# Sketched attention and a squared-ReLU layer on one core: full PE tiles, three batches repeated by DMA, a written order

## Chip, cores and metric

The kernel runs on one core of a Trainium2 chip. The metric is device microseconds of one execution. TensorE (PE) multiplies, with weight loads shown apart as PEld; VectorE is DVE, ScalarE is ACT, GpSimd is POOL, and SyncE (SP) issues most DMAs.

## What is computed

There are 4 batches of 4 heads, 1088 tokens, 32 dimensions, R = 8 sketch rows. Attention's output (4352 tokens of 128 values) goes through a layer of 2048 hidden units.

```
phi(x)  = (S1 x) outer (S2 x)                # 64 features per token
kv, z   = sum_t phi(k_t) v_t , sum_t phi(k_t)
x       = (phi(q) kv) / (phi(q) z + 1e-6)    # per head; heads side by side
out     = (relu(x w_in))^2 w_out             # 128 -> 2048 -> 128
```

Attention runs in f32, the layer in bf16.

## The kernel before

`attention(b, ...)` adds the operations of one batch to a graph and `ffn(n, ...)` those of one token block: `SIZES` has 320, seven of 512, and 448. Each operation has a name, the engines that may do it, a cost and a due value. `Graph.run` simulates the engines with these costs and gives the order, once, when the kernel is built; each engine then executes its list in that order.

For one batch the names are these. The loads `ldk`, `ldq`, `ldv` bring K, Q, V. `tk` and `tq` transpose 32 x 32 blocks on DVE. `ksk` (L448) sketches 32 tokens of keys per matmul; `ka` copies one sketch on ACT and `kp` (L466) makes the 64 products. `vp` (L420) packs V beside a column of ones on POOL. `kv` (L485) sums products with V, in pieces of 32 features; `kve` copies the result to `kvz`, and for two batches a second time with its halves swapped to `kvs`.

The queries' features take one of two ways (`MODE`). Batches 0 and 1 ("pe"): `qr` (L528) makes both sketches already repeated to 64 features, with the stationary `SR`; `qa` copies one of them on ACT, `qp` (L546) multiplies on DVE. Batches 2 and 3 ("dma"): `qr` (L559) makes the plain sketches, `ab` (L568) copies them to SBUF, `wr` (L573) stores them to DRAM (`scr`), `rdA` (L582) and `rdB` (L589) read them back repeated into `qp` and `Bq`, and `qp` (L602) multiplies these.

`num` (L626) multiplies 32 tokens by `kvz`; `mx` divides (L651 to L655), `tx` (L667) transposes and `xe` (L672) copies to `xT`. In a block, `m1` (L693) makes 128 hidden units per matmul, `r` (L702) is the relu of two such, `g` (L712) their square, `m2` (L718) adds to one accumulator `o0`; `oe` (L725) transposes it and `st` (L735) stores it. An f32 matmul appears in the trace as two loads and two matmuls.

SP issues its DMAs one after the other, and each waits until the one eight places before it on the hardware queues has ended. Weights come through POOL's queue, after `gate`, which waits for K of batch 0.

Of the kernel before, what the change touches and what calls it, by code (L numbers as in the profile page):

```python
# [15 lines left out]
SEM = 0.035  # L16
SWITCH = 0.095
LOOK = 0.12
LANES = 8
DMA_FIRST = 1.3  # L20
DMA_LAST = 0.75


KSPLIT = False
N_HEAT = 7
W_PARTS = ((0, 1), (1, 2), (2, 4))
K_LOADS = ((0, 16), (16, 34))
Q_LOADS = ((0, 10), (10, 34))
MODE = ("pe", "pe", "dma", "dma")
QGROUPS = (((0, 10), (10, 22), (22, 34)), ((0, 12), (12, 24), (24, 34)), ((0, 24), (24, 34)), ((0, 24), (24, 34)))  # L30
LD_PRI = ({"k": -200, "q": -198.5, "v": -199}, {"k": -30, "q": -29, "v": -28}, {"k": -20, "q": -25, "v": -19}, {"k": -10, "q": -15, "v": -9})
RD_PARTS = ((0, 768), (768, 1088))
LATE = 10
RELU_PEN = 0.6
SQ_PEN = 0.3
SIZES = [320] + [512] * 7 + [448]
STAGE = {"tk": 1, "ksk": 2, "ka": 3, "kp": 4, "kv": 5, "vp": 5, "kve": 7, "tq": 2.5, "qr": 4, "qa": 4.5, "qp": 6, "num": 8,
         "mx": 9, "tx": 9.5, "xe": 10, "wr": 4.6, "rd": 4.7}
FIRST = {"tk": -50, "ksk": -49, "ka": -48, "kp": -46, "kv": -44, "vp": -44, "kve": -43, "tq": -47.5, "qr": -45, "qa": -44.5,
         "qp": -43.5, "num": -42, "mx": -41, "tx": -40, "xe": -39}  # L40
LEAD = 14.0
MARG = 3.0


def VT(b, key):
    if b == 0:
        return FIRST[key]
    s1 = 17.0 * b - MARG
    lead = LEAD + (6.0 if MODE[b] == "dma" and key in ("tq", "qr", "qa", "wr", "rd") else 0.0)
    return s1 - lead + lead * STAGE[key] / 12.0  # L50

CRIT = {"tk0.0", "tk0.1", "ksk0.0", "ksk0.1", "ka0.0", "ka0.1", "kp0.0", "kp0.1", "kv0.0", "kv0.1", "kve0.0", "kve0.1", "kve0.2", "kve0.3",
        "tq0.0", "qr0.0", "qa0.0.0", "qa0.0.1", "qp0.0.0", "qp0.0.1", "num0.0", "mx0.0", "tx0.0", "xe0.0", "m1.0.0"}
CRIT_LOOK = 1.0


class Buf:
    def __init__(self, *kinds):
        self.kinds = kinds
        self.slot = None  # L60
        self.banks = ()
        self.pending = 0


class Op:
    def __init__(self, name, alts, fn, deps, pri, alloc, uses, shape, dma, after):
        self.name, self.alts, self.fn, self.pri = name, alts, fn, pri
        self.deps = [d for d in deps if d is not None]
        self.after = [d for d in after if d is not None]
        self.alloc, self.uses = list(alloc), list(alloc) + list(uses)  # L70
        self.shape, self.dma = shape, dma
        self.look = LOOK
        self.start = self.end = self.eng = None


class Graph:

    def __init__(self, slots):
        self.ops = []
        self.free = {}
        self.kinds = {}
        for kind, names in slots.items():
            self.kinds[kind] = [(n, parts) for n, parts in names]
            for _, parts in names:
                for x in parts:  # L90
                    self.free[x] = [0.0, None]

    def add(self, name, alts, fn, deps=(), pri=0.0, alloc=(), uses=(), shape=None, dma=None, after=()):
        op = Op(name, alts, fn, deps, pri, alloc, uses, shape, dma, after)
        for b in op.uses:
            b.pending += 1
        self.ops.append(op)
        return op

    def slot_time(self, buf, taken=()):  # L100
        best = None
        for kind in buf.kinds:
            for name, parts in self.kinds[kind]:
                if any(x in taken for x in parts) or any(self.free[x][1] is not None and self.free[x][1].pending for x in parts):
                    continue
                t = max(self.free[x][0] for x in parts)
                if best is None or t < best[0] - 0.3:
                    best = (t, name, parts)
        return best

    def run(self):
        eng_free, pipe, shape = {}, 0.0, None
        lanes = []
        todo = {id(o): len(o.deps) + len(o.after) for o in self.ops}
        succ = {}
        for o in self.ops:
            for d in o.deps + o.after:
                succ.setdefault(id(d), []).append(o)
        ready = [o for o in self.ops if todo[id(o)] == 0]
        order = []  # L120
        while ready:
            cands = []
            for o in ready:
                t_slot = 0.0
                ok = True
                taken = []
                for b in o.alloc:
                    s = self.slot_time(b, taken)
                    if s is None:
                        ok = False  # L130
                        break
                    taken += s[2]
                    t_slot = max(t_slot, s[0] + SEM)
                if not ok:
                    continue
                best = None
                for e, (busy, lat, *pen) in o.alts.items():
                    pen = pen[0] if pen else 0.0
                    t = max(eng_free.get(e, 0.0), t_slot)
                    for d in o.deps:  # L140
                        t = max(t, d.end + (SEM if d.eng != e else 0.0))
                    for d in o.after:
                        t = max(t, d.start)
                    if o.dma is not None and e != "POOL" and len(lanes) >= LANES:
                        t = max(t, lanes[-LANES])
                    if e == "PE" and o.shape != shape:
                        t += SWITCH
                    if best is None or t + lat + pen < best[0]:
                        best = (t + lat + pen, t, e, busy, lat)
                cands.append((best[1], o, best))  # L150
            assert cands, "no operation can start: " + ", ".join(o.name for o in ready[:20])
            t0 = min(c[0] for c in cands)
            _, o, (_, t, e, busy, lat) = min(
                (c for c in cands if c[0] <= t0 + c[1].look), key=lambda c: (c[1].pri, c[0]))
            for b in o.alloc:
                _, b.slot, b.banks = self.slot_time(b)
                for x in b.banks:
                    self.free[x] = [t, b]
            o.start, o.end, o.eng = t, t + lat, e
            if o.dma is not None:  # L160
                pipe = max(pipe, t + busy - 0.4 + DMA_FIRST) + o.dma
                o.end = pipe + DMA_LAST
                if e != "POOL":
                    lanes.append(o.end)
            if e == "PE":
                shape = o.shape
            eng_free[e] = t + busy
            for b in o.uses:
                b.pending -= 1
                for x in b.banks:  # L170
                    self.free[x][0] = max(self.free[x][0], o.end)
            ready.remove(o)
            order.append(o)
            for s in succ.get(id(o), ()):
                todo[id(s)] -= 1
                if todo[id(s)] == 0:
                    ready.append(s)
        assert len(order) == len(self.ops)
        self.order = sorted(order, key=lambda o: o.start)
        return self.order  # L180


def act(n):
    return (0.833e-3 * n + 0.053, 0.833e-3 * n + 0.18)


def dve(n, rate=1.042e-3, fix=0.07):
    return (rate * n + fix, rate * n + fix + 0.09)


def pool(n, rate=2.1e-3):
    return (rate * n + 0.12, rate * n + 0.16)


def pe(t):
    return (t, t + 0.17)
# [3 lines left out]
def kernel(  # L200
# [30 lines left out]
    NB = 2  # L231
    NR = 4
# [9 lines left out]
    for i in range(3):  # L242
        for j in range(2):
            tiles[f"h{i}.{j}"] = tiles[f"h{i}"][:, 512 * j : 512 * j + 512]
    for n in ("a0", "o0"):
        tiles[n] = ps.tile([128, 512], F32, name=n, tag=n)
# [543 lines left out]
```

## Time and profile before

| | |
|---|---|
| median of 3 runs | 131.54 us (129.92 to 133.82) |
| profiled execution, span | 132.4 us |
| PE, PEld busy | 103.6, 59.0 us |
| DVE, ACT, POOL busy | 93.4, 81.9, 12.8 us |
| bytes moved by DMA | 15.29 MB, mean 115 GB/s |

The profiled execution is known by its span, from the first to the last instruction; no other time of it was taken. It lies 0.9 us over the median of the runs. The groups of instructions name a line, an engine and an operation, then the number of instructions, busy us and the mean ns of one, and the idle time before them with what ended it. In the chain of waits a row is start, duration and what ran; "issue" is time for which the profile shows no cause. In the table by stretches each engine has its busy us and, in brackets, its instructions; the last three columns are the granted PE clock, the DMA share and GB/s.

### The profile page before, as it was taken

To read this page: it belongs to the slowest core of one execution; us is meant where nothing else is said; L and a number is where in the kernel's file an instruction comes from. 1 tells how busy PE (TensorE), PEld (TensorE's weight loads), DVE (VectorE), ACT (ScalarE), POOL (GpSimd) and SP (SyncE) were. 2 spreads that over 40 slices of the span, in tenths; PEclk is the share of its full clock that TensorE was granted. 3 is DMA by queue.
4 is the path that set the end of the run, shared out by engine and by line. 5 is a ranking of instruction groups with operands and counts; after the bars stand their busy time and mean duration, and the time that the engine had idled before them with its cause. 6 is when DMAs were issued, how large, how long until landed. Compare 5 with 4: busy or idle time off the path is not lost.

```text
span 132.4 us, 4611 instructions
## 1 busy us (share of the span) xinstructions
PE 103.6 (78%) x1979; PEld 59.0 (45%) x1995; DVE 93.4 (71%) x155; ACT 81.9 (62%) x117; POOL 12.8 (10%) x38
## 2 busy tenths in 40 slices
PE   6375297691578898999998699999939789999940
PEld 2074164460544455554553454455434444445410
DVE  2546079795029999889953994997299567899950
ACT  0412017940139896989869419989850299999910
POOL 5492005050310000000000000000000000000000
PEclk9999558999689999999999999999995999999996
DMA  4989999994000030149856306595650220040314
GB/s 120 270 196 341 246 288 301 230 274 94 6 0 5 0 57 7 47 135 242 155 132 160 55 5 124 133 241 153 159 118 5 44 40 0 0 68 11 54 30 69
DMA packets 26596, 15.29 MB, mean 115 GB/s; under 512 B 19792, under 2 KB 24272, under 8 KB 26576
## 3 DMA queue, kind: packets, MB, share of 16 engines
q1 hardware_dynamic: 25152, 13.67, 42.5%
q0 software_dynamic: 992, 1.05, 5.1%
q8 instruction: 15, 0.25, 0.8%
q10 hardware_dynamic: 432, 0.28, 0.7%
q14 instruction: 5, 0.04, 0.1%
HBM read 13.25 MB, written 2.79 MB: 121 GB/s over the span
## 4 chain that ended last, share of the span: by engine, by line
PE 39%; DVE 22%; issue 12%; ACT 10%; DMA 9%; SPq 4%; ACTq 2%; DVEq 0%
PE o L718 10%; DVE g L712 9%; PE h L693 9%; ACT r L702 8%; DVE kp L466 6%; DMA Bq<-scr 5%; PE h L626 4%; PE a L626 3%; PE h L667 3%; SPq L589 3%; DMA S_sb<-in_S_dram 3%; PE a L448 2%; PE h L485 2%; DVE osb L725 2%; PE a L485 2%
## 5 line engine op out<-in xcount | busy, mean ns | idle before, releaser
L702 ACT ACTIVATE r<-h 128x1024 bf16<-128x1024 f32 (+2 forms) x68 | 61.3, 1000 | 5.7 <-PE h L693 5.1
L712 DVE TENSOR_TENSOR g<-r 128x1024 bf16<-128x1024 bf16 (+2 forms) x64 | 40.5, 668 | 6.1 <-ACT r L702 5.3
L718 PE MATMUL o<-g,w_out 128*128 128x512 bf16 (+2 forms) x135 | 38.8, 375 | 3.3 <-DVE g L712 2.0
L693 PE MATMUL h<-xT,w_in 128*128 128x512 bf16 (+2 forms) x137 | 37.9, 369 | 3.9 <-ACT xT L672 1.4
L693 PEld LDWEIGHTS <-w_in 128*128 128x128 bf16 x144 | 15.7, 114 | 18.1 <-issue 6.9
L718 PEld LDWEIGHTS <-w_out 128*128 128x128 bf16 x144 | 13.2, 99 | 18.3 <-issue 8.0
L672 ACT COPY xT<-h 128x768 bf16<-128x768 bf16 (+2 forms) x4 | 2.5, 626 | 14.6 <-PE h L667 14.6
L485 PE MATMUL a<-vp,kp 128*32 128x33 f32 x432 | 5.8, 207 | 4.4 <-issue 4.4
L602 DVE TENSOR_TENSOR qp<-qp,Bq 128x1536 f32<-128x1536 f32 (+1 forms) x4 | 5.2, 1288 | 5.3 <-DMA Bq<-scr 5.3
L485 PEld LDWEIGHTS a<-vp,kp 128*32 128x32 f32 x432 | 5.0, 118 | 6.6 <-issue 6.2
L626 PE MATMUL h<-kvz,qp 128*32 128x66 f32 x260 | 6.1, 242 | 2.2 <-ACT r L702 2.1
L541 ACT COPY A<-h 128x384 f32<-128x384 f32 (+1 forms) x12 | 4.9, 465 | 3.8 <-PE h L528 3.7
L725 DVE STREAM_TRANSPOSE osb<-o 128x512 f32<-128x512 f32 (+2 forms) x9 | 6.1, 682 | 1.5 <-PE o L718 1.5
L710 ACT ACTIVATE g<-r 128x640 bf16<-128x640 bf16 (+1 forms) x8 | 7.1, 900 | 0.1
L420 POOL COPY vp<-vin 128x512 f32<-128x512 f32 x8 | 5.0, 648 | 20.8 <-DMA vin<-in_v_dram 18.7
L626 PEld LDWEIGHTS h<-kvz,qp 128*32 128x32 f32 x260 | 5.2, 122 | 3.8 <-ACT r L702 3.0
L466 DVE TENSOR_TENSOR kp<-h,ka 128x1280 f32<-128x1280 f32 (+1 forms) x4 | 5.7, 1422 | 1.2 <-PE h L485 1.0
L433 DVE STREAM_TRANSPOSE kT<-kin 128x1088 f32<-128x1088 f32 (+2 forms) x5 | 5.3, 1069 | 1.5 <-DMA kin<-in_k_dram 1.5
L466 DVE TENSOR_TENSOR kp<-a,ka 128x1024 f32<-128x1024 f32 (+1 forms) x4 | 5.1, 1285 | 1.5 <-ACT ka L458 1.5
L528 PE MATMUL h<-qT,SR 32*64 32x192 f32 (+1 forms) x192 | 5.9, 358 | 0.2 <-DVE r L704 0.2
L546 DVE TENSOR_TENSOR qp<-h,A 128x384 f32<-128x384 f32 (+1 forms) x12 | 5.9, 518 | 0.0
L485 PE MATMUL h<-vp,kp 128*32 128x33 f32 x144 | 2.4, 230 | 4.4 <-issue 2.7
(61 smaller groups left out, 88.5 us busy)
## 6 DMA issues: line engine op xcount, KB each, us to landing
vin<-in_v_dram SPq DMA_DIRECT2D x14, 128.0 KB
kin<-in_k_dram SPq DMA_DIRECT2D x3, 544.0 KB
qin<-in_q_dram SPq DMA_DIRECT2D x3, 544.0 KB
qp<-scr SPq DMA_DIRECT2D x4, 384.0 KB
Bq<-scr SPq DMA_DIRECT2D x8, 192.0 KB
out_dram<-osb SPq DMA_DIRECT2D x16, 64.0 KB
qp<-scr SPq DMA_DIRECT2D x4, 160.0 KB
Bq<-scr SPq DMA_DIRECT2D x8, 80.0 KB
```

What stands on the lines that cost most here:

```text
L433: nc.vector.transpose(kT[i][:, 32 * c0 : 32 * c1], kin[i][:, 32 * c0 : 32 * c1])
L466: nc.vector.tensor_tensor(out=kp[i][:, j0:j1].rearrange("p j h (x y) -> p (j h) x y", y=R), in0=bb[:, :, None, :].to_broadcast([128, m, R, ...
L485: nc.tensor.matmul(t[p : p + 32, 33 * (h // 2) : 33 * (h // 2) + 33], kp[i][:, j, h, 32 * f : 32 * f + 32], vp[i][:, h, j, :], start=(j == ...
L528: nc.tensor.matmul(at(hb[h // 2])[lo : lo + 64, 512 * half + 256 * x : 512 * half + 256 * x + n], SR[32 * h : 32 * h + 32, x].rearrange("p ...
L546: nc.vector.tensor_tensor(out=qp[i][:, pr, t0 : t0 + 2 * n].rearrange("p (m s) -> p m s", m=2), in0=at(hb[pr]).rearrange("p (m s) -> p m s ...
L626: nc.tensor.matmul(t[32 * cc : 32 * cc + 32, 2 * pr : 2 * pr + 2, :], qp[i][:, pr, 32 * c : 32 * c + 32], (kvs if sw else kvz)[i][:, pr], ...
L693: nc.tensor.matmul(at(hb)[:, step * w : step * w + N], w_in[:, 512 * (ct // E) : 512 * (ct // E) + 512].rearrange("p (c e) -> p e c", e=E) ...
L702: nc.scalar.activation(o, view(at(hb)), ACTF.Relu)
L710: nc.scalar.activation(at(gb)[:, 0 : W * N], r, ACTF.Square)
L712: nc.vector.tensor_tensor(out=at(gb)[:, 0 : W * N], in0=r, in1=r, op=ALU.mult)
L718: nc.tensor.matmul(at(ob)[:, 0:N], w_out[:, ct, :], at(gb)[:, N * w : N * w + N], start=(ct == 0), stop=(ct == CT - 1))
L725: nc.vector.transpose(at(sbuf)[:, 0:N], at(ob)[:, 0:N])
```

## The change

1. **Full tiles.** `ksk` takes 128 tokens per matmul (four of 32 before), `num` 128 tokens (four of 32), `kv` a head's 64 features (two pieces of 32). For this `tk` writes K so that 128 tokens lie side by side, and `kvs` is gone. `qr` of batch 0 takes two heads per matmul with a masked `SR`.
2. **Queries.** Batch 0 alone keeps the PE way, in tiles of 256 tokens. Batches 1 to 3 take the DMA way: one matmul makes both sketches, and the repeats go in two halves (`HALVES`, 18 and 16 chunks of 32 tokens). `rdA` reads the SBUF tile `ab` directly; only the second sketch goes through DRAM.
3. **First loads.** `S0` and the first four quarters of V come from ACT's queue, `S1` from POOL's, K and Q from SP's.
4. **Blocks.** 256, 512, 320, five of 512, 448, 256. Two relus share one square (2048 columns) in the blocks of `Q` = 2; blocks of 256 take four hidden tiles per relu (`W` = 4). All eight PSUM banks are four tiles `h0` to `h3`, and their halves `b0` to `b7`; `m2` accumulates in `b6` and `b7` by turns.
5. **Order.** `Graph.run` is gone. A table `PLAN` names each operation, its engine and its buffer.

```diff
-SIZES = [320] + [512] * 7 + [448]
+BLOCKS = ((256, 4, 1), (512, 2, 2), (320, 2, 2)) + ((512, 2, 2),) * 5 + ((448, 2, 2), (256, 4, 1))
+GROUPS = (((0, 8), (8, 16), (16, 24), (24, 34)),) + (((0, 18), (18, 34)),) * 3
+QTILES = ((0, 8), (8, 16), (16, 24), (24, 32), (32, 34))
+HALVES = ((0, 18), (18, 34))
+PLAN = """
+zero:DVE ldk0.0:SP S1:POOL z0:POOL mk:DVE tk0.0:DVE iota:POOL ident:DVE
...
+        for line in PLAN.split():
+            name, eng, *slots = line.split(":")
...
+            o.fn(eng)
...
             def f_ksk(e, j0=j0, j1=j1, kab=kab):
...
-                    for g in range(4):
-                        c = tok(j, g)
-                        nc.tensor.matmul(
-                            o[32 * g : 32 * g + 32, :, j - j0, :], kT[i][:, 32 * c : 32 * c + 32],
-                            SK.rearrange("p x h r -> p x (h r)"), start=True, stop=True)
+                    lo = 128 * j if j < 8 else 960
+                    nc.tensor.matmul(o[:, :, j - j0, :], kT[i][:, lo : lo + 128],
+                                     SK.rearrange("p x h r -> p x (h r)"), start=True, stop=True)
...
-                        for f in range(2):
-                            p = 64 * (h % 2) + 32 * f
-                            nc.tensor.matmul(
-                                t[p : p + 32, 33 * (h // 2) : 33 * (h // 2) + 33],
-                                kp[i][:, j, h, 32 * f : 32 * f + 32], vp[i][:, h, j, :],
+                        nc.tensor.matmul(
+                            t[64 * (h % 2) : 64 * (h % 2) + 64, 33 * (h // 2) : 33 * (h // 2) + 33],
+                            kp[i][:, j, h, :], vp[i][:, h, j, :],
...
+                            nc.tensor.matmul(
+                                at(hb)[64 * u : 64 * u + 64, 512 * w : 512 * w + n], SK.rearrange("p x h r -> p (x h r)"),
+                                qT[i][:, s0 : s0 + n], start=True, stop=True)
...
+                        dma[e].dma_start(out=qp[i][:, pr, s0 : s0 + n],
+                                         in_=row(u, 0, 2 * pr)[0:16, None, 0:n].to_broadcast([16, R, n]))
...
+                    dma[e].dma_start(out=scr[i][u, :, 0:n], in_=row(u, 1, 0)[0:32, 0:n])
...
-                        for cc in range(4):
-                            c = c0 + 4 * x + cc
-                            if c >= c1:
-                                c -= 2
-                            sw = swap and 2 * (c - c0) >= c1 - c0
-                            nc.tensor.matmul(
-                                t[32 * cc : 32 * cc + 32, 2 * pr : 2 * pr + 2, :],
-                                qp[i][:, pr, 32 * c : 32 * c + 32], (kvs if sw else kvz)[i][:, pr],
-                                start=True, stop=True)
+                        nc.tensor.matmul(t[0:n, 2 * pr : 2 * pr + 2, :], qp[i][:, pr, lo : lo + n], kvz[i][:, pr],
+                                         start=True, stop=True)
```

PE at the front, before: after the warm-up matmuls come batch 0's key sketches (`SK,kT_107`), kv in two runs (`vp_115,kp_119`) around query sketches, and num (`kvz_121,qp_125`).

```order
L448 MATMUL a_66<-SK,kT_107 32x2x32 x16
L448 MATMUL h_65<-SK,kT_107 32x2x32 x20
L485 MATMUL h_65<-vp_115,kp_119 32x33 x32
...
L485 MATMUL h_65<-vp_115,kp_119 32x33 x40
L626 MATMUL a_66<-kvz_121,qp_125 32x66 x9
L626 MATMUL a_66<-kvs_123,qp_125 32x66 x3
```

The same place in the change; `h_63` to `h_66` are the tiles `h0` to `h3`, and the line numbers are those of the new file.

```order
L360 MATMUL h_63<-SK,kT_102 128x2x32 x9
L416 MATMUL h_64<-qT_104,SR 128x256 x4
L386 MATMUL h_63<-vp_108,kp_112 64x33 x16
L266 LDWEIGHTS zero
L266 MATMUL h_66<-zero 128x512
...
L386 MATMUL h_63<-vp_108,kp_112 64x33 x20
L360 MATMUL h_63<-SK,kT_103 128x2x32 x5
L501 MATMUL h_63<-kvz_114,qp_116 128x66 x4
```

Nine key sketches stand for 36, 36 matmuls of kv for 72, and five key sketches of batch 1 now stand between kv and num of batch 0.

SP's queue around the first batch that is repeated by DMA, before (batch 2: `ab_129`, `scr_131`):

```order
L573 DMA scr_131<-ab_129 32x2x272 x4
L582 DMA qp_125<-scr_131 128x1x768 x2
L582 DMA qp_125<-scr_131 128x1x320 x2
L735 DMA out_dram<-osb_81 32x16x32 x4
L589 DMA Bq_127<-scr_131 64x1x768 x4
L589 DMA Bq_127<-scr_131 64x1x320 x4
L735 DMA out_dram<-osb_86 32x8x32 x8
```

And in the change (batch 1: `ab_121`, `scr_123`):

```order
L463 DMA scr_123<-ab_121 32x576
L323 DMA vin_107<-in_v_dram 32x4x256
L303 DMA qin_100<-in_q_dram 128x1088
L323 DMA vin_107<-in_v_dram 32x4x256
L331 DMA vp_109<-in_v_dram 32x4x32 x2
L459 DMA qp_117<-ab_121 128x1x576 x2
L469 DMA Bq_119<-scr_123 64x1x576 x4
L463 DMA scr_123<-ab_121 32x512
L303 DMA kin_99<-in_k_dram 128x1088
L596 DMA out_dram<-osb_69 32x8x32
L323 DMA vin_106<-in_v_dram 32x4x256 x4
L469 DMA Bq_119<-scr_123 64x1x512 x4
```

No store stands between the repeats of one half; loads of V, Q and K of other batches do.

More of the change, by code (lines that the diff above doesn't have):

```diff
@@ L42 @@
[L42 to L53, printed above, removed]
@@ L57 @@
+st6.2624.2:SP m2.9.1:PE g.9.2:ACT:g0 st6.2624.3:SP m2.9.2:PE g.9.3:DVE:g2 m2.9.3:PE st7.3136.0:SP
+oe9:DVE:osb2 st7.3136.1:SP st7.3136.2:SP st7.3136.3:SP st7.3264.0:SP st7.3264.1:SP st7.3264.2:SP st7.3264.3:SP
+st8.3648.0:SP st8.3648.1:SP st8.3648.2:SP st8.3648.3:SP st9.4096.0:SP st9.4096.1:SP st9.4096.2:SP st9.4096.3:SP
+warm:ACT
+"""
 class Buf:
@@ L100, in slot_time @@
[L100 to L180, printed above, removed]
@@ L183, in act, with __init__, add @@
[L183 to L196, printed above, removed]
+    def __init__(self):
+        self.ops = {}
+    def add(self, name, engines, fn, deps=(), alloc=(), uses=(), after=(), **info):
+        assert name not in self.ops, name
+        self.ops[name] = Op(name, engines, fn, deps, after, alloc, uses, info)
+        return self.ops[name]
@@ L256, in at @@
         return tiles[buf.slot]
+    dma = {"SP": nc.sync, "ACT": nc.scalar, "POOL": nc.gpsimd}
+    NB = 2
     eps = 1e-6
@@ L417, in attention @@
+        def f(e):
+            for c in range(2):
+                dma[e].dma_start(out=vp[i][64 + 32 * c : 96 + 32 * c, :, NJ - 1, 0:D], in_=vsrc[:, :, 32 + c, :])
+        o_vt = add(f"ldv{b}.t", "SP", f, [z_ops[i]] + prev(b, "kv"), kind="dma", kb=32, key="vt")
         for a in range(2):
@@ L713, in ffn @@
-            o3 = add(f"g.{n}.{m}", {"DVE": dve(W * N, 0.521e-3, 0.05), "ACT": act(W * N + 40) + (SQ_PEN,)}, f_g, [o2], p - 0.6, alloc=[gb], uses=[rb])
-            def f_m2(e, m=m, gb=gb):
-                for w in range(W):
-                    ct = W * m + w
-                    nc.tensor.matmul(at(ob)[:, 0:N], w_out[:, ct, :], at(gb)[:, N * w : N * w + N],
-                                     start=(ct == 0), stop=(ct == CT - 1))
-            last = add(f"m2.{n}.{m}", {"PE": pe(W * (N / 2400 + 0.0027))}, f_m2, [o3, wo, last], p - 0.7,
-                       alloc=[] if m else [ob], uses=[gb, ob] if m else [gb])
+                    nc.vector.tensor_tensor(out=at(gb)[:, 0 : Q * W * N], in0=r, in1=r, op=ALU.mult)
@@ new lines, in ffn, with f_m2 @@
+            o3 = add(f"g.{n}.{m}", "DVE ACT", f_g, relus, alloc=[gb], uses=[rb], n=Q * W * N, kind="sq")
+            for mm in range(m - Q + 1, m + 1):
+                def f_m2(e, mm=mm, gb=gb):
+                    for w in range(W):
+                        ct = W * mm + w
+                        lo = N * (W * (mm % Q) + w)
+                        nc.tensor.matmul(at(ob)[:, 0:N], w_out[:, ct, :], at(gb)[:, lo : lo + N],
+                                         start=(ct == 0), stop=(ct == CT - 1))
+                wo = o_wout[wpart(W * mm + W - 1)]
+                last = add(f"m2.{n}.{mm}", "PE", f_m2, [o3, wo, last], alloc=[] if mm else [ob], uses=[ob, gb] if mm else [gb],
+                           kind="mm", mm=[(128, N, 1)] * W)
```

616 lines of the change are left out of this document (281 added, 335 removed).

## Prediction

> **What bounds the kernel now.** I read the engine totals first, then stretches of the span, the chain that ended last, and then the gaps on each engine.
>
> ```profile
> PE 103.6 (78%) x1979; PEld 59.0 (45%) x1995; DVE 93.4 (71%) x155; ACT 81.9 (62%) x117; POOL 12.8 (10%) x38
> q8 instruction: 15, 0.25, 0.8%
> ...
> 0.00:21.60 21.60, 12.64 (x350) 8.30 (x351) 10.65 (x23) 4.49 (x12) 9.10 (x30) 0.84 0.94 253
> 21.60:42.00 20.40, 13.27 (x450) 9.42 (x442) 12.24 (x19) 10.31 (x24) 3.72 (x9) 0.92 0.50 117
> 42.00:72.00 30.00, 28.48 (x493) 15.22 (x499) 25.29 (x45) 26.31 (x35) 0.00 (x0) 1.00 0.44 99
> 72.00:106.00 34.00, 28.46 (x604) 16.15 (x611) 26.72 (x42) 20.45 (x27) 0.00 (x0) 0.95 0.47 105
> 106.00:126.30 20.30, 19.73 (x93) 9.67 (x93) 17.21 (x27) 20.30 (x23) 0.00 (x0) 1.00 0.19 31
> 126.30:132.40 6.10, 1.04 (x5) 0.26 (x3) 1.27 (x2) 0.00 (x0) 0.00 (x0) 0.79 0.26 44
> ```
>
> The columns after the stretch are PE, PEld, DVE, ACT and POOL busy. No one engine bounds the whole. Until 42 us, a third of the span, no engine is busy for two thirds of the time; from 42 to 72 PE, DVE and ACT are all nearly full; from 72 to 106 DVE and ACT fall back; then ACT is full until the last relu at 126.3, and 6.1 us are tail. What can be won is therefore idle time at the front and between 72 and 106. Work saved on one engine alone is worth little where three are nearly full.
>
> Of the front, the chain that ended last says this:
>
> ```profile
> 12.23 0.60 PE h L485 x41
> 12.84 2.73 issue
> 15.57 0.71 PE h L485 x33
> ...
> 16.88 1.62 PE a L626 x48
> ...
> 21.01 0.43 PE h L693 x2
> ...
> 30.25 4.38 issue
> 34.63 1.27 PE a L485 x70
> ...
> 35.95 1.32 PE h L626 x47
> ```
>
> Twice PE stops in the middle of one run of equal small matmuls (kv, L485) with nothing to wait for that the profile shows, for 2.73 and 4.38 us. PE has 1979 + 1995 = 3974 instructions and q8 brought 0.25 MB in 15 packets, so a packet is about 260 of them. The DMA view of two stretches, 13.0 to 13.2 and 31.8 to 32.0 us, shows one packet of q8 in each, 2.4 and 2.6 us before PE goes on:
>
> ```profile
> q8 instruction: 1, 0.02, 29.3%
> q8 instruction: 1, 0.02, 41.7%
> ```
>
> I read both stops as PE waiting for its instructions, which it had used up in tiny matmuls.
>
> [...]
>
> **The change, part by part.**
>
> *Front: -3.0.* In the new order PE has 284 f32 matmuls instead of 832. At four records each (two loads, two matmuls), and two for each bf16 one, that is 1874 records for 3990: half the blocks. Up to the first m1 I count about 300, where the old kernel stopped after some 440. The stop at 12.84 should go; at 15.57 PE went on for 0.71, so kv of batch 0 ends 13.6 at the latest and, with fewer, wider matmuls, I say 12.9, not 16.28. From there to the first m1 at 21.01 now pass 4.7 us: kv's copy, num, division, query sketches, transposes, xT's copy. The new order has the same with five key sketches of batch 1 more (5 x 0.17 as priced below, 0.17 that a group adds, and a warm-up matmul: 1.2) and less at half clock (num at 16.88 took 1.62, the same 48 records 0.90 in the rows below): 4.7 + 1.2 - 0.8 = 5.1, so the first m1 at 18.0 us, 3.0 earlier. Bounds: 0, if the loads of V come late instead, and -5. S1 on the POOL queue and V's quarters on ACT I cost at nothing: no row shows a small load on POOL, and ten warm-up matmuls stand ahead of the first key sketch in any case.
>
> *Second stop: -5.5.* The 4.38 us go, and with them the half clock behind them: kv and num at 34.63 and 35.95 took 2.59 us, where the rows below give 0.90 + 0.90 at full clock. That is 6.1 in all; I leave 0.6 for batch 1's V, which loads late in both. Bounds: -6.1, and 0 if V takes the stop's place.
>
> *Repeats by DMA: -4.0.* Batches 2 and 3 now wait for their repeated queries:
>
> ```profile
> 54.41 1.74 SPq L573 DMA_DIRECT2D scr<-ab  x4
> 59.67 2.32 SPq L735 DMA_DIRECT2D out_dram<-osb  x4
> 62.03 5.79 SPq L589 DMA_DIRECT2D Bq<-scr  x8
> 71.60 1.76 DVE L602 TENSOR_TENSOR qp<-qp,Bq 128x1536 f32<-128x1536 f32 x1 [2.63 <-DMA Bq<-scr]
> 74.01 0.59 PE L718 MATMUL o<-g,w_out 128*128 128x512 bf16 x2 [1.81 <-DVE g L712]
> 78.85 0.80 ACT L672 COPY xT<-h 128x768 bf16<-128x768 bf16 x1 [4.54 <-PE h L667]
> 98.12 2.04 PE L626 MATMUL h<-kvz,qp 128*32 128x66 f32 x96 [2.12 <-ACT r L702]
> 104.48 0.80 ACT L672 COPY xT<-h 128x768 bf16<-128x768 bf16 x1 [6.83 <-PE h L667]
> ```
>
> From the first store of the copy ab at 54.41 to the product at 71.60 a batch needs 17.2 us, with four stores ahead of the Bq repeats. PE loses 1.81 + 2.12 = 3.9 us, ACT 4.54 + 6.83 = 11.4. In the change the first 18 of 34 chunks are repeated and used apart, half A comes from the tile ab itself, and ab2 and ab3 stand far ahead of their use. The bounds are 0 and 11.4; I take PE's 3.9, because PE will be the fullest. For batch 1 the same path is new: behind ab1, ACT has ten relus of 1024 columns, seven of 640, two squares and some copies before block 3's first relu, about 18 us at 0.93 and 0.65 us a relu, against 17.2 for a whole batch and less for its first half. It just fits, at no cost.
>
> ```profile
> 57.46 8.39 ACT L702 ACTIVATE r<-h 128x1024 bf16<-128x1024 f32 x9 [0.38 <-PE h L693]
> 41.25 1.29 ACT L702 ACTIVATE r<-h 128x640 bf16<-128x640 f32 x2
> ```
>
> *Squares in pairs: -1.0.* A square of 1024 columns takes 683 ns and one of 896 takes 617, so 1024 more columns are 0.53 us. A pair is 1.21 instead of 1.37, and 27 pairs on DVE save 4.2. DVE is on the path only in part; I take 1.0 (bounds 0 and 4.2).
>
> ```profile
> L712 DVE TENSOR_TENSOR g<-r 128x1024 bf16<-128x1024 bf16 x52 | 33.7, 683 | 4.1 <-ACT r L702 3.9 <-PE o L718 0.2
> L712 DVE TENSOR_TENSOR g<-r 128x896 bf16<-128x896 bf16 x8 | 4.8, 617 | 0.6 <-PE o L718 0.2
> ```
>
> *Full PE tiles: +5.5.* This part I expect to cost time. Now four matmuls of 32 columns run side by side; one of 128 columns does their work in the same number of steps.
>
> ```profile
> 25.98 0.77 PE L448 MATMUL h<-SK,kT 128*32 128x64 f32 x40 [0.75 <-DVE xs L655]
> 29.58 0.65 PE L448 MATMUL h<-SK,kT 128*32 128x64 f32 x32
> 74.53 1.60 PE L626 MATMUL h<-kvz,qp 128*32 128x66 f32 x96
> 77.46 0.90 PE L626 MATMUL a<-kvz,qp 128*32 128x66 f32 x48
> 90.16 0.77 PE L485 MATMUL a<-vp,kp 128*32 128x33 f32 x64
> 91.97 0.90 PE L485 MATMUL a<-vp,kp 128*32 128x33 f32 x80
> L448 PEld LDWEIGHTS h<-SK,kT 128*32 128x32 f32 x40 | 0.6, 110 | 1.1 <-DVE xs L655 1.1
> L528 PEld LDWEIGHTS h<-qT,SR 32*64 32x64 f32 x32 | 0.6, 131 | 0.3 <-issue 0.3
> ```
>
> Eight records are one step of four matmuls. A step of ksk costs (0.77 - 0.65) = 0.12 us, of num (1.60 - 0.90)/6 = 0.115, of kv (0.90 - 0.77)/2 = 0.065. The steps stay 9, 18 and 18 a batch. A weight load of 32 columns takes 110 ns and one of 64 takes 131: 21 ns for each 32 columns, so 86 ns for 128, and two per matmul are 0.17 us. If loads run beside matmuls but not beside each other, a step costs the longer of the two: 0.17, 0.17 and (64 columns) 0.086. That is 0.5 + 1.0 + 0.4 = 1.9 us a batch, 7.6 in all. Batch 0's query sketches use two row tiles instead of eight (about +1.6), batch 1's fall from three groups to one (-1.5). Of 7.7 I put 5.5 on the path, since other engines share it. Bounds: 0, if all loads hide, and the exposed case below.
>
> [...]
>
> *Tail and the rest: 0.* Two alternating output accumulators replace one; no long wait on it stands in the rows, so I cost it at nothing. The last block is smaller (256 columns), but its square, matmuls, transpose and stores follow as before.
>
> **Sum.** 132.4 - 3.0 - 5.5 - 4.0 - 1.0 + 5.5 = 124.4 us for a span. The profiled 132.4 is 0.9 above the median of the runs, 131.54, so I predict 123.5 us.
>
> **Rivals.**
>
> *Loads hide wholly.* bf16 matmuls of all 128 rows run without a gap though a load stands before each (two more m1 matmuls cost 1.02 - 0.59 = 0.43 us). If f32 does the same at full width, the +5.5 is nothing: 118.
>
> ```profile
> 61.30 0.59 PE L693 MATMUL h<-xT,w_in 128*128 128x512 bf16 x2
> 62.20 1.02 PE L693 MATMUL h<-xT,w_in 128*128 128x512 bf16 x4
> ```
>
> *Late operands.* The order is a list written ahead, SP takes it in turn, and the first repeat of batch 1 stands behind 544 KB of queries and 0.25 MB of V. If so, the 4.0 are not won and batch 1 adds a wait like the 2.63 us for Bq above: 123.5 + 4.0 + 2.6 = 130, no change. For it speaks that batch 1 only just fits, and that w_in's second part is now issued behind vp0.1; against it that each later batch has more room.
>
> *Loads exposed: slower.* If an f32 load of all columns cannot run beside the matmul before it, each step costs 0.11 + 0.17 (kv 0.055 + 0.086): +0.17 on 9, +0.17 on 18, +0.08 on 18, or 6 us a batch, 24 in all and 26 with the query sketches. PE is then the bound; with 3/4 of it on the path, 19.5 in place of 5.5, the time is 137.5. It is slower from about 16 us on the path, which is 0.09 us a step over the 180 steps. For it: no row shows an f32 load of 128 columns. Against it: the narrow f32 loads do hide, since a step of num is 0.115 with eight loads of 110 ns in it.
>
> [...]
>
> **How the numbers follow.** Forecast (119 to 129) 0.46, loads hidden (118) 0.22, late operands (130) 0.14, loads exposed (137.5) 0.18. A measurement here tells about 2% from no change: 128.9 to 134.2. Faster is 0.46 + 0.22 = 0.68, same 0.14, slower 0.18. The range 113 to 134 leaves out most of the exposed case and a little below 113.
>
> **What would show it.** Right: no "issue" stop of over 1 us on PE in kv, q8 at about half its bytes, first m1 near 18, no granted clock of half after 15 us, ksk of five matmuls at 0.17 us a step, and DVE waits for Bq under 1 us. Wrong: num at 0.28 us a step, DVE waiting for Bq or qp in batch 1, or the first m1 after 20.

## Result and the profile after

The changed kernel takes 141.7 us (median of 5 runs, 141.36 to 146.23) where the kernel before took 131.54 (129.92 to 135.72): 1.084 times as long, 95% interval 1.072 to 1.096. The prediction was 123.5 us and faster: wrong in sign. Medians are of all runs of a kernel, while a ratio compares only those within some 1.5% of its fastest, and is left blank where too few remain.

The profiled execution of the change took 142.91 us, 1.2 over its median, for a span of 141.1. That of the kernel before is known by its span of 132.4 alone. In its other executions the time is some 2 us over the span, so by estimate it took 134.4, which is 2.9 over the median and not 0.9.

The page of the changed kernel: engine totals, the granted PE clock in 40 slices of 3.5 us, the queue that brings instructions.

```profile
PE 120.1 (85%) x937; PEld 81.0 (57%) x937; DVE 91.6 (65%) x144; ACT 82.0 (58%) x103; POOL 13.3 (9%) x31
PEclk9955555599999999999999999999999999999999
q8 instruction: 7, 0.11, 0.3%
```

PE has half the records, 1874 for 3974, and is busy for 16.5 us more. q8 fell from 15 packets (the prediction's "blocks") to 7. The clock is half from the third slice to the eighth, 0.50 from 7.6 to 28.0 us.

The same in stretches (PE, PEld, DVE, ACT, POOL busy; granted clock, DMA share, GB/s):

```profile
0.00:21.00 21.00, 16.20 (x117) 11.12 (x118) 8.83 (x24) 2.43 (x4) 7.94 (x25) 0.68 0.88 219
21.00:29.40 8.40, 7.48 (x36) 5.16 (x35) 3.09 (x6) 2.15 (x6) 0.00 (x0) 0.58 0.07 12
29.40:42.00 12.60, 11.75 (x98) 9.46 (x97) 7.61 (x16) 7.54 (x11) 0.73 (x2) 1.00 0.39 92
42.00:72.00 30.00, 26.68 (x289) 19.07 (x287) 22.75 (x28) 20.96 (x31) 4.66 (x5) 1.00 0.76 192
72.00:106.00 34.00, 31.50 (x253) 20.65 (x253) 26.72 (x39) 25.39 (x29) 0.00 (x0) 1.00 0.58 123
```

PE's timeline at the front (start, us, instructions; in brackets the idle time before and what ended it):

```profile
6.17 1.10 PE L360 MATMUL h<-SK,kT 128*128 128x64 f32 x8 [1.21 <-DVE SK L236]
8.89 2.39 PE L360 MATMUL h<-SK,kT 128*128 128x64 f32 x10 [1.61 <-DVE kp L374]
...
13.22 1.22 PE L416 MATMUL h<-qT,SR 64*128 64x256 f32 x4 [0.78 <-ACT A L424]
14.37 1.92 PE L386 MATMUL h<-vp,kp 128*64 128x33 f32 x32
...
19.47 2.40 PE L360 MATMUL h<-SK,kT 128*128 128x64 f32 x10
22.43 1.98 PE L501 MATMUL h<-kvz,qp 128*128 128x66 f32 x8 [0.56 <-ACT kvz L397]
24.20 0.63 PE L266 MATMUL h<-zero 128*128 128x512 bf16 x1
24.76 2.93 PE L416 MATMUL h<-qT,SR 64*128 64x256 f32 x12
...
29.44 0.63 PE L547 MATMUL h<-xT,w_in 128*128 128x256 bf16 x4
```

The first m1 starts at 29.44 us; it was forecast at 18.0 and stood at 21.01. From there to the end pass 111.7 us, before 111.4. So between these two executions all that was lost lies ahead of the first m1, and all that was to be won behind it was lost again. (Their spans differ by 8.7 us, the medians by 10.2; the difference has no place in the rows.) And the second row is odd: a key sketch of batch 0's second half waits for `kp` of the first half, whose data it does not touch.

Waits by engine and line (total, times, longest):

```profile
PE h L578 <- DVE osb L586: 3.8, 4, 1.4
PE h L523 <- DVE xs L513: 1.6, 2, 1.1
PE h L360 <- DVE kp L374: 1.6, 1, 1.6
PE h L578 <- DVE kp L374: 1.0, 1, 1.0
SPq L463 <- ACT ab L448: 28.9, 2, 23.2
```

The first row is as odd: a block's output matmuls (m2) wait for the transpose `osb` of the block before, though the two accumulators alternate. The last: SP stood at the store of `ab1` from 12.5 to 35.8 us. SP's wait eight places back shows before in `SPq L403 <- DMA qin<-in_q_dram: 2.0, 1, 2.0`: a load of V starts at 25.37 us, when the load of Q that SP issued at 17.86 us, eight DMAs earlier, has landed.

### The profile page after: what moved, and what is told of

Its sections match the earlier page's. It is cut to its first block, busy times and chain, and to the rows that moved or that the text cites. A ratio compares the mean times of both kernels' runs of the same rounds, so it can differ in the third digit from the quotient of the medians.

```text
span 141.1 us, 2509 instructions
## 1 busy us (share of the span) xinstructions
PE 120.1 (85%) x937; PEld 81.0 (57%) x937; DVE 91.6 (65%) x144; ACT 82.0 (58%) x103; POOL 13.3 (9%) x31
## 4 chain that ended last, share of the span: by engine, by line
PE 38%; DVE 12%; issue 5%; SPq 4%; DMA 3%; ACT 1%; DVEq 0%; ACTq 0%
PE h L578 15%; PE h L547 12%; DVE g L571 5%; PE h L501 4%; PE h L386 4%; DMA Bq<-scr 3%; DVE kp L374 2%; SPq L469 2%; DVE osb L586 2%; SPq L463 1%; PE h L442 1%; DVE qp L479 1%; DVE r L560 1%; PE h L523 1%; PE h L360 1%
## 5 line engine op out<-in xcount | busy, mean ns | idle before, releaser
L578 PE MATMUL h<-g,w_out 128*128 128x512 bf16 (+3 forms) x160 | 39.8, 347 | 6.8 <-DVE osb L586 3.8
L547 PE MATMUL h<-xT,w_in 128*128 128x512 bf16 (+3 forms) x160 | 39.8, 348 | 0.5 <-DVE r L560 0.4
L571 DVE TENSOR_TENSOR g<-r 128x2048 bf16<-128x2048 bf16 (+3 forms) x33 | 34.8, 1085 | 1.4 <-PE h L578 1.3
L501 PE MATMUL h<-kvz,qp 128*128 128x66 f32 x144 | 18.2, 283 | 0.6 <-ACT kvz L397 0.6
L501 PEld LDWEIGHTS h<-kvz,qp 128*128 128x128 f32 x144 | 17.7, 199 | 1.5 <-ACT kvz L397 0.8
L374 DVE TENSOR_TENSOR kp<-h,ka 128x1024 f32<-128x1024 f32 (+1 forms) x8 | 10.8, 1353 | 6.5 <-ACT ka L367 6.5
L360 PE MATMUL h<-SK,kT 128*128 128x64 f32 x72 | 11.3, 318 | 2.9 <-DVE kp L374 1.6
L386 PEld LDWEIGHTS h<-vp,kp 128*64 128x64 f32 x288 | 11.2, 159 | 3.7 <-issue 2.9
L360 PEld LDWEIGHTS h<-SK,kT 128*128 128x128 f32 x72 | 10.6, 230 | 3.9 <-DVE kp L374 1.8
L386 PE MATMUL h<-vp,kp 128*64 128x33 f32 x288 | 11.8, 241 | 1.1 <-DVE xT L528 1.1
L569 ACT ACTIVATE g<-r 128x2048 bf16<-128x2048 bf16 (+2 forms) x7 | 10.5, 1497 | 0.0
L397 ACT COPY kvz<-h 64x66 f32<-64x66 f32 x6 | 1.3, 208 | 10.8 <-PE h L360 8.9
```

The source lines that it names most:

```text
L360: nc.tensor.matmul(o[:, :, j - j0, :], kT[i][:, lo : lo + 128], SK.rearrange("p x h r -> p x (h r)"), start=True, stop=True)
L374: nc.vector.tensor_tensor(out=kp[i][:, j0:j1].rearrange("p j h (x y) -> p (j h) x y", y=R), in0=bb[:, :, None, :].to_broadcast([128, m, R, ...
L386: nc.tensor.matmul(t[64 * (h % 2) : 64 * (h % 2) + 64, 33 * (h // 2) : 33 * (h // 2) + 33], kp[i][:, j, h, :], vp[i][:, h, j, :], start=(j ...
L501: nc.tensor.matmul(t[0:n, 2 * pr : 2 * pr + 2, :], qp[i][:, pr, lo : lo + n], kvz[i][:, pr], start=True, stop=True)
L547: nc.tensor.matmul(at(hb)[:, step * w : step * w + N], w_in[:, 512 * (ct // E) : 512 * (ct // E) + 512].rearrange("p (c e) -> p e c", e=E) ...
L569: nc.scalar.activation(at(gb)[:, 0 : Q * W * N], r, ACTF.Square)
```

## The experiments

| | median | ratio to before | first m1 | from there to the end |
|---|---|---|---|---|
| before | 131.5 | | 21.0 | 111.4 |
| the change | 141.7 | 1.084 (1.072 to 1.096) | 29.4 | 111.7 |
| e1 narrow f32 tiles | 134.1 | 1.029 (1.016 to 1.042) | 23.9 | 107.9 |
| e2 warm-ups in gaps | 135.6 | 1.041 (1.027 to 1.054) | 23.0 | 110.9 |
| e3 front's PSUM tiles apart | 138.2 | 1.053 (1.039 to 1.066) | 23.9 | 111.3 |
| e4 SP's order | 142.0 | 1.093 (1.082 to 1.104) | 28.2 | 111.7 |
| e5 e1 to e4 | 133.1 | | 20.8 | 109.6 |
| e6 e5, kv wide | 129.2 | 0.999 (0.990 to 1.009) | 21.0 | 106.2 |
| e7 e5, all wide | 135.6 | 1.051 (1.034 to 1.067) | 22.0 | 111.3 |
| e8 before, num wide | 135.5 | | 21.5 | 113.1 |
| e9 before, kv wide | 129.9 | 0.981 (0.970 to 0.992) | 19.5 | 107.6 |
| e10 e6, m1 early | 128.6 | 0.979 (0.972 to 0.987) | 17.9 | 107.6 |
| e11 e6, SP as changed | 129.6 | 0.988 (0.980 to 0.995) | 22.3 | 105.5 |
| e12 e9, warm-ups | 129.9 | 0.982 (0.965 to 0.998) | 18.3 | 108.4 |
| e13 e10, accumulators apart | 123.9 | (before: 132.6) | 19.1 | 103.1 |
| e14 e13, all wide | 125.8 | 0.966 (0.960 to 0.972) | 18.8 | 105.3 |
| e15 the change, tiles apart only | 126.6 | 0.969 (0.963 to 0.976) | 22.1 | 103.1 |

The last two columns are of the profiled execution; that of e8 was its longest, 136.69 us.

**e1, narrow tiles.**

```diff
-nc.tensor.matmul(o[:, :, j - j0, :], kT[i][:, lo : lo + 128], ...
+for g in range(4):
+    nc.tensor.matmul(o[32*g : 32*g+32, :, j - j0, :], kT[i][:, lo+32*g : lo+32*g+32], ...
```

`num` and `kv` likewise, in pieces of 32.

> The changed kernel with its order kept, but key sketches and numerators again as four matmuls of 32 tokens and kv as two of 32 features. Theory W (the wide f32 tiles cost PE its loads, and PE is the bound behind 37 us): num falls from 0.22 us a step to about 0.115, ksk from 0.24 to 0.12, kv from 0.105 to 0.065, which is 1.9 + 1.1 + 0.7 = 3.7 us a batch and 11 us for batches 1 to 3 alone; with a front that is some 2 us shorter, 141.7 becomes 128 to 131. Rival O (the loss is the new order: the front's waits and the queue of SP): at most 4 us go, 138 to 142. Rival F (narrow tiles bring back stops in which PE waits for its instructions, 2.7 and 4.4 us in the kernel before): PE work falls as in W, q8 goes from 7 packets to about 15, and "issue" stops of over 2 us appear; 133 to 137.

134.1 us: 7.6 less. The spans differ by 9.3; 5.5 of these lie ahead of the first m1 and only 3.8 behind, where W expected 11. F's stop is there too, 2.27 us that end in "issue", with 14 packets of q8 where the change has 7:

```profile
16.86 0.29 PE L390 MATMUL h<-vp,kp 128*32 128x33 f32 x11 [2.27 <-issue]
```

**e2, warm-ups in the gaps.** The warm-up matmuls `heat13` to `heat17` go ahead of `ksk0.0`, `heat18` to `heat23` behind it.

> The changed kernel with eleven more warm-up matmuls on PE, five ahead of batch 0's first key sketch and six behind it, where PE stands idle for 1.21 and 1.61 us. Theory C (the half clock from 7.8 to 28.0 us, which begins behind these gaps, is a large part of the front's loss): the granted clock stays at full, 19 us of PE work at the front shrink towards 10, the first m1 comes at 21 to 23 instead of 29.4, and the time is 133 to 136. Rival S (the front is a chain of waits, so that the clock hardly matters): first m1 after 27, 139 to 142. A third way: the clock falls later all the same, since matmuls with short moving operands keep PE busy in the records but not its clock; then the half clock only moves by some us, and the time by 0 to 3.

Theory C: first m1 at 23.00, and 6.1 us less in all. In the stretch from 8 to 21 us, first of the change, then of e2, PE is as busy at half clock with 99 records as at full clock with 131:

```profile
8.00:21.00 13.00, 11.33 (x99) 8.91 (x100) 5.34 (x6) 0.88 (x2) 4.19 (x10) 0.50 1.00 232
```

```profile
8.00:21.00 13.00, 11.09 (x131) 7.96 (x130) 7.05 (x10) 2.49 (x8) 3.96 (x9) 1.00 0.92 222
```

**e3, front's tiles apart; e4, SP's order.**

```diff
-ksk0.1:PE:b1 ... ksk1.0:PE:b1 ... num0.0:PE:b0 ... heat12:PE:b6
+ksk0.1:PE:b4 ... ksk1.0:PE:b5 ... num0.0:PE:b7 ... heat12:PE:b1
```
```diff
-wr1.0:SP ... ldv1.02:SP ... ldq2.0:SP ... ldv1.03:SP ... ldv1.t:SP
+ldv1.02:SP ldv1.03:SP ldv1.t:SP ldq2.0:SP wr1.0:SP
```

> The changed kernel with three PSUM buffers moved: the second key sketch of batch 0, the first of batch 1 and the first numerators each get a tile of their own instead of the other half of a tile in use, and one warm-up matmul gives way. No instruction is added or moved. Theory P (the halves of one PSUM tile wait for each other: the second sketch stood 1.61 us for kp on the other half, the copy ka of batch 1 2.06 us for the numerators): these waits go, the first m1 comes 2 to 4 us earlier, 138 to 140. Rival: the waits are covered by PE work that stands ahead anyway; first m1 within 1 us of 29.4, time within 1 us of 141.7.

> The changed kernel with four loads (two quarters and the tail of V of batch 1, Q of batch 2) issued on SP ahead of the store of ab1 that stood from 12.5 to 35.8 us. Theory Q (the blocked queue makes V, Q and K of batches 1 to 3 late and costs time): vp of batch 1 runs before 20 us instead of 41.3, kv and the repeats of batch 1 come earlier, 137 to 140. Rival (PE is full behind 37 us, idle for 9 us in all, so that earlier operands buy nothing): vp runs early all the same, the time stays within 1 us of 141.7.

e3: the second key sketch runs on behind the first,

```profile
5.02 2.19 PE L360 MATMUL h<-SK,kT 128*128 128x64 f32 x18
23.89 0.63 PE L547 MATMUL h<-xT,w_in 128*128 128x256 bf16 x4
```

first m1 5.5 us earlier, median 3.5 less (the spans differ by 5.9): theory P, and larger at the first m1 than it said. Part of that is the clock, 0.63 from 8 to 21 us where the change has 0.50. e4: V of batch 1 is packed at 23.0 instead of 41.3 us (first the change, then e4), and the time is the same. Theory Q falls.

```profile
41.27 1.17 POOL L336 COPY vp<-vin 128x512 f32<-128x512 f32 x2 [25.27 <-DMA vp<-in_v_dram]
```

```profile
23.04 1.17 POOL L336 COPY vp<-vin 128x512 f32<-128x512 f32 x2 [7.58 <-DMA vin<-in_v_dram]
```

e11 repeats the question on e6, with the same answer (129.6 for 129.2).

**e5, e6, e7: all mended, with three widths.** Narrow; kv wide; all wide. Eleven warm-up matmuls stand in the gaps at 7.8 to 15.5 us.

> The changed kernel with all of it mended at once: narrow key sketches, numerators and kv (as in e1), the PSUM buffers apart (e3), SP's four loads ahead of the store (e4), and eleven warm-up matmuls put where PE stands idle at the front (three behind the first query sketch, four ahead of kv, two in it, two ahead of the first numerators). Theory W+C+P (wide tiles, half clock and shared tiles are separate parts of one loss at the front): the first m1 comes at 18 to 20 us instead of 29.4, and from there to the end pass 106 to 108 us as in e1 (107.9): 125 to 128, faster than before by 3% or more. Rival F (with narrow tiles PE has to wait for its instructions, as the 2.27 us in e1 show): first m1 at 21 to 23, 129 to 131. Rival L (a chain of waits sets the first m1 whatever PE does): as e1, 23 to 24, 131 to 133.

> As e5, but kv stays at 64 features a matmul: 288 f32 matmuls of four records fewer. Theory W: kv costs 0.04 us a step more, 0.7 a batch, so 1 to 3 us more than e5. Rival F (the stops for instructions matter more than kv's loads): no stop of over 2 us on PE, and 1 to 3 us less than e5.

> As e5, but with all full tiles of the changed kernel. By theory W+C+P the first m1 comes 1 to 2 us later than in e5 (wide ksk, kv and num at full clock cost some 2 us more in batch 0) and the rest takes 111 us as in the changed kernel: 130 to 133, 4 to 6 us over e5. If the width matters only through the half clock, it is within 1.5 us of e5.

In all three the first m1 is back near the 21.0 of before (20.8 to 22.0); behind it e7 still takes 111.3 us, as the change does. e7 is no faster than e2 (135.6 both), which has the warm-ups alone, and its first m1 comes only 1.0 us earlier. This suggests that with the clock held the front's shared tiles cost little more, so that the two losses at the front are largely one. e5, with 15 packets of q8, has three stops of 1.15 to 1.58 us that end in "issue":

```profile
60.41 0.60 PE L390 MATMUL h<-vp,kp 128*32 128x33 f32 x26 [1.55 <-issue]
71.55 0.27 PE L390 MATMUL h<-vp,kp 128*32 128x33 f32 x7 [1.58 <-issue]
97.46 0.28 PE L506 MATMUL h<-kvz,qp 128*32 128x66 f32 x2 [1.15 <-issue]
```

e6, with 12 packets, has no such stop and takes 3.8 us less (3.2 by the spans), so F holds for kv. The price of a step comes from two runs of `num` each, first the change (20 and 36 records, 10 and 18 steps), then e6 (80 and 144, the same steps):

```profile
57.00 2.40 PE L501 MATMUL h<-kvz,qp 128*128 128x66 f32 x20
104.42 4.13 PE L501 MATMUL h<-kvz,qp 128*128 128x66 f32 x36
```

```profile
46.81 1.37 PE L504 MATMUL h<-kvz,qp 128*32 128x66 f32 x80
91.60 2.32 PE L504 MATMUL h<-kvz,qp 128*32 128x66 f32 x144
```

(4.13 - 2.40) / 8 = 0.216 us for a wide step, (2.32 - 1.37) / 8 = 0.119 for a narrow one. Nine steps of `ksk` took 2.17 and 1.21 us (0.107 more each). A step of wide kv is 0.12, (1.36 - 1.12) / 2 in these rows of e10, where a narrow one was 0.065:

```profile
10.57 1.12 PE L388 MATMUL h<-vp,kp 128*64 128x33 f32 x32 [0.56 <-POOL vp L336]
12.60 1.36 PE L388 MATMUL h<-vp,kp 128*64 128x33 f32 x40
```

That is 72 x 0.097 + 36 x 0.107 + 72 x 0.055 = 14.8 us of PE. From e6 to e7, where `ksk` and `num` are wide (10.8 us), 6.4 us came out. All three widths together, e5 to e7, cost 2.5 us by the medians and 2.9 by the spans, since narrow kv brings its stops.

**e8, e9, e12: parts of the change in the kernel before.** `num` of batches 2 and 3 with 128 tokens; kv with 64 features; that with eight warm-ups in the front's gaps.

> The kernel before with one part of the change: numerators of batches 2 and 3 in matmuls of 128 tokens, 16 of 18 steps a batch, with the planned order left as it is. Theory W (0.22 us a step for a full f32 tile instead of 0.115): PE gets 32 x 0.105 = 3.4 us more work, num of 64 matmuls takes 3.5 us instead of 1.9; what of it is not covered by PE's waits around these batches (1.8 + 2.1 us before) is lost: 0 to 3.4 us slower, I say 1.5. Rival (the full tiles are slow only in the changed kernel's order): num stays near 0.12 to 0.17 a step and the time within 0.5 us of before.

> The kernel before with one part of the change: kv with a head's 64 features a matmul, 288 f32 matmuls instead of 576, 1152 PE instructions of 3974 fewer; the planned order is left. Theory F (PE's stops of 2.73 and 4.38 us are waits for instructions): the stops in kv go or shrink, q8 falls from 15 packets to about 11, and kv costs 0.04 us a step more on 72 steps, 2.9 us, part of it covered: 125 to 129. Rival G (the stops had another cause, such as a transfer that fills the DMA engines): the stops stay where they were and the time is 132 to 134.

> The kernel before with kv at 64 features (e9) and eight warm-up matmuls where PE stands idle at its front: four ahead of batch 0's first kv, two ahead of its second, two ahead of its first numerators. In e9 the granted clock was half from 8.5 to 18.1 us and the first m1 came at 19.47. Theory C (the clock falls where PE's work is thin, and dense matmuls in the gaps hold it): full clock through the front, first m1 at 17 to 18 us; if the rest follows, 126 to 129, 1 to 2.5 us under e9 (129.9). Rival (the chain to the first m1 hangs on other engines, or the start buys little, as from e6 to e10, where 3.2 us at the first m1 gave 0.6 us): within 0.7 us of e9.

e8 is inconclusive in time: four stops of 1.8 to 3.5 us that end in "issue" stood in its profiled run. It has 3606 records of PE and PEld where the kernel before has 3974 and only two stops over 1 us, so their number alone does not set the stops. Its steps are as wide there as in the change (2.79 us for 12, 1.00 for 4: 0.22). e9 shows F: with 3399 records, 575 fewer, the 2.73 us stop is gone and the 4.38 us one is down to

```profile
29.70 0.54 PE L448 MATMUL h<-SK,kT 128*32 128x64 f32 x23 [1.52 <-issue]
```

and the kernel takes 1.9% less (0.970 to 0.992, from two of its six runs), though a step of kv takes 0.115 us there, (1.36 - 1.13) / 2, for 0.065. Its forecast, like that of e6, took records for matmuls: wide kv saves 144 f32 matmuls, so 576 instructions and not 1152. e12: the granted clock is 0.9 or more in every slice up to 28 us, the first m1 comes 1.2 us earlier, and nothing is gained.

**e10, first m1 ahead of the sketches.**

```diff
-qr0.8.1:PE ... qr0.16.0:PE:h2 ... tx0.0:PE:b0 xe0.0:ACT ... qr0.16.1:PE qr0.24.0:PE:h3 ... m1.0.0:PE:h0
+qr0.8.1:PE tx0.0:PE:b0 xe0.0:ACT ... m1.0.0:PE:h0 qr0.16.0:PE:h2 r.0.0:ACT:r0 ... qr0.16.1:PE qr0.24.0:PE:h3
```

> e6 with the first transposes and the first m1 on PE moved ahead of the query sketches that stand before them (two of 256 tokens and half of a third), the copies of xT and the first relu on ACT likewise; the work is the same. In e6 batch 0's first division ended at 17.1 us, its transposes ran at 19.2 behind those sketches, m1 at 21.0. Theory A (the written order makes the first m1 wait): first m1 at 18 to 18.5 us, 2.5 to 3 us earlier. If the layer's work behind it is what the end hangs on, the time falls by 1.5 to 3 us against e6 (129.2), to 126 to 128. Rival: the batches' operands or ACT are reached in the same order as ever, so the start buys nothing: within 0.7 us of e6.

> e6 with SP's order as in the changed kernel: the store of ab1 stands ahead of V of batch 1 and Q of batch 2. In the changed kernel (e4) moving these loads bought nothing. Theory: with less PE work the late operands are no longer hidden; vp of batch 1 comes behind 30 us again, PE waits for Bq or qp by 1 to 2 us as in e1, and the time is 1 to 3 us over e6. Rival (still hidden): within 0.7 us of e6.

First m1 at 17.86, near the 18.0 forecast for the change, though with narrow tiles and more warm-ups. The time is 0.6 us less than e6 by the medians and 1.7 by the spans, nearer the rival than theory A. The sketches only moved behind it. So an early first m1 did not bring the forecast time. Behind it PE still stood 3.8 us for `osb`, as in the change:

```profile
PE h L582 <- DVE osb L590: 3.8, 4, 1.4
PE h L582 <- DVE g L575: 1.8, 2, 1.5
PE h L388 <- DVE xT L532: 1.8, 1, 1.8
PE h L527 <- DVE xs L517: 1.6, 2, 1.1
PE h L582 <- DVE kp L376: 1.5, 2, 1.2
```

**e13, e14, e15: no shared tile for the accumulators.**

```diff
-for i in range(4):     # h0 to h3, halves b0 to b7
+for i in range(3):     # h0 to h2, halves b0 to b5
...
+for i in (6, 7):
+    tiles[f"b{i}"] = ps.tile([128, 512], F32, name=f"o{i}", tag=f"o{i}")
```

What lay on `h3` moves: `qr0.24` and `qr1` to `h1`, `num0.8`, `num0.16` and `tx0.8` to `b6`, `b7`, `b6`; `b6` and `b7` change parts. The memory is the same.

> e10 with the two output accumulators as tiles of their own instead of halves of one tile h3, and what else lay on h3 moved (two query sketches to h1, two numerators and a transpose to the accumulators' tiles). The prediction cost the two accumulators at nothing. Theory P2: halves of one tile wait for each other here too. In e10 PE stood 0.73 + 1.42 + 0.90 + 0.74 = 3.8 us with the first output matmuls of a block, which write one half, for the transpose osb that reads the other, and 1.17 + 0.33 us for kp, which reads the other half. These 5.3 us go, and 2 to 4 us of them reach the end: 125 to 127. Rival: they only cover for waits on relus and squares that come next, and the time stays within 0.7 us of e10 (128.6).

> e13 with full tiles for key sketches and numerators again, as in the changed kernel; everything else as e13. This prices the width where no tile is shared and the clock is held. Wide tiles are 10.8 us of PE work more (0.10 us a step on 72 steps of num and 36 of ksk). From e6 to e7 6.4 us of it reached the end; e13 has fewer waits on PE, so I expect as much or more: 130 to 134. Rival (PE's rest idle time takes it up): under 127.

> The changed kernel with its PSUM tiles set apart as in e3 and e13 and nothing else: wide tiles, SP's order, thirteen warm-up matmuls and the first m1 behind the sketches as they were. Theory P2 (shared tiles cost the changed kernel twice, at the front and at every block's end): 3.5 us as in e3 and 4.7 us as from e10 to e13, 133 to 135, the same as before or a little slower. Rival (in the changed kernel wide tiles keep PE so full that the accumulators' waits are covered): 137 to 138.5, as e3.

e13: 123.9 (its six runs go from 119.79 to 125.72), beyond the 125 to 127 of P2. e15 settles that the shared tiles are the cause: the changed kernel, its wide tiles, its SP order and its written order as they were (but for the sketch and numerators moved with their tiles), with no tile shared in these places, takes 126.6 us, 15.1 less than the change and faster than before by 3.1%. PE's waits by line, of e15:

```profile
PE h L418 <- ACT A L426: 1.6, 3, 0.8
PE o L580 <- DVE g L573: 1.6, 1, 1.6
PE h L388 <- POOL vp L338: 1.5, 1, 1.5
PE o L268 <- DVE mk L227: 1.2, 1, 1.2
PE h L388 <- DVE xT L530: 1.1, 1, 1.1
PE h L418 <- DVE kp L376: 1.1, 1, 1.1
```

The rows for `osb` and for `ksk` behind `kp` are gone, and from 72 to 106 us PE, at 31.50 in the change, now hardly rests:

```profile
72.00:106.00 34.00, 33.69 (x202) 21.12 (x204) 29.95 (x45) 28.43 (x32) 0.00 (x0) 1.00 0.57 116
```

Of the 15.9 us that the span lost 7.3 lie ahead of the first m1 and 8.6 behind it. Behind it the clock is the same in both (1.00 and 0.99), so the 8.6 are the tiles' own. Ahead of it the clock was half for 20 us in the change and full in e15 (1.00 from 0 to 21 us), so the 7.3 are tiles and clock together. But the clock cannot be all of it: the run of e15 with the lowest mean clock, 0.925, took 130.94 us, and the change's profiled one, with 0.926, took 142.91.

Two more pairs agree. e3 had moved the front's tiles alone; from e3 to e15 the span loses 10.0 us, 8.2 of them behind the first m1. PE's rows of e3 for `osb` and `kp` make 4.4 of these; the rest was not followed. e7 and e14, both wide and at nearly full clock (0.996 and 0.993), differ in the tiles and the early m1: 135.6 and 125.8 us, where the early m1 had brought 0.6 to 1.7 (e6, e10).

e14, at 125.8, comes out as its rival said. The width of `ksk` and `num` where no tile is shared in these places, e13 to e14, costs 1.9 us by the medians and by the spans, but 5.9 against e13's shortest run; and e13's profiled execution has one stop of 1.56 us that ends in "issue", which e14's has not:

```profile
58.92 0.31 PE L506 MATMUL h<-kvz,qp 128*32 128x66 f32 x5 [1.56 <-issue]
```

So this price is not settled, nor whether the shared tiles made the width dearer. Theory W, with which the study began, is the smaller part in any case: at most 6.4 us (e6, e7) of `ksk` and `num`, where the tiles brought 15.1, the clock with them.

## Why the prediction was wrong, step by step

- **Tail and the rest, 0.** This step failed, and with it the front. "Two alternating output accumulators replace one; no long wait on it stands in the rows, so I cost it at nothing." They are halves of one tile, and the program waits by tile: `m2` into one half stands for `osb` of the other, 3.8 us in the change. The rows show the same for the key sketch behind `kp`, 1.6 us. Behind the first m1 the forecast left 106.4 us (124.4 - 18.0); measured were 111.7, and 103.1 with no tile shared in these places (e15). So what the step put at nothing was 8.6 us. The diff shows the halves, and the prediction names them; it did not ask which operations meet on one tile.
- **Front, -3.0.** It came out as +8.4: the first m1 at 29.4 instead of 18.0, the largest miss. 7.3 us of these 11.4 are the shared tiles and the half clock together (e15: 22.1). The half clock lasted 20 us and began at 7.6 us, in the second of PE's gaps (1.61 us, up to 8.89); warm-ups in the gaps alone brought the first m1 to 23.0 (e2). Another 3.2 are the query sketches that the order puts ahead of m1 (e6 to e10, and e7 to e14). With these out of the way and wide tiles it came at 18.84 (e14), so the other pieces of the sum were near.
- **Second stop, -5.5.** The forecast of the stops was right: none over 1 us, q8 at 0.11 MB for 0.25; e1 and e5 bring stops back with more instructions, and in the kernel before e9 takes one away and shortens the other to 1.52 us. That PE waits for its instructions there is my reading of the one packet of q8 in each of the two stops before; no run shows it apart, and e8 has four stops with fewer records. The sum was not: 4.38 and the 0.79 at half clock (2.59 - 1.80) make 5.2, not 6.1. What the term was worth was not tried alone.
- **Repeats by DMA, -4.0.** DVE waits 0 us for `Bq` (5.3 before), batch 1 included; SP's blocked queue cost nothing (e4, e11), so the rival of late operands falls. But the two rows of PE that gave the 3.9 us do not name the repeats: one waits for a square, the other for a relu. What this part was worth was not tried alone.
- **Squares, -1.0.** DVE's squares take 34.8 us instead of 40.5, ACT's 10.5 instead of 7.1; not tried alone.
- **Full PE tiles, +5.5.** The sign was right. PE's work was undersized, 14.8 us for 7.6: the step is 0.216, not 0.17, and for kv 0.12, not 0.086, since I took the difference of two load durations for a rate. The part on the path was 6.4 us for `ksk` and `num` with shared tiles (e6, e7) and from 1.9 to 5.9 without (e13, e14). The term took loads to run one after the other, and those of `num` overlap in the change: 144 of 199 ns on the mean make 28.7 us, and PEld was busy with them for 17.7. What sets the 0.216 was not shown. The rival of exposed loads (0.28 a step) came near in time by another cause.
- **The sum.** 123.5 us was forecast. With only the shared tiles taken out it is 126.6 (e15). So one thing left out cost 15.1 us, with the half clock in it, and the rest missed by 3.1. That this is so near is in part luck: the first m1 of e15 comes 4.1 us later than forecast and 3.3 us less pass behind it.

## What to carry to other kernels

Where buffers are given out by hand, ask of each pair of halves who reads the one while another engine writes the other: in this program waits go by the whole tile (3.8 us for `osb`, 1.6 and 1.0 for `kp` in the change), and a double buffer inside one tile is none. A row in which an instruction waits for something whose data it doesn't use was the sign of it; move the buffer before you price anything else. The same matmul width cost 6.4 us with such waits in place (e6, e7) and 1.9 by the medians without (e13, e14), though e13's runs lie too far apart to settle it. So price a part again once such waits are gone.

## What was not expected of the hardware

The granted clock stayed at 0.50 from 13.2 to 21.9 us in the change, though PE was busy by its records for 8.65 of these 8.70 us; it rose at 28.0, behind twelve records of sketches with 256 columns. Being busy in the records was thus not enough to lift it. e3 and e15 have the same front on PE, in the same order, and the clock of 8 to 21 us was 0.63 in the one and 1.00 in the other:

```profile
8.00:21.00 13.00, 11.24 (x105) 8.84 (x105) 6.29 (x10) 1.18 (x4) 3.95 (x9) 0.63 0.96 230
```

```profile
8.00:21.00 13.00, 8.94 (x119) 6.67 (x120) 8.14 (x11) 2.76 (x8) 4.40 (x10) 1.00 0.97 226
```

PE was busy for 11.24 of these 13 us at 0.63 and for 8.94 at 1.00. What sets the clock was not shown.
